# Nyström attention into a squared-ReLU feed-forward: C v on eight tiles, C and A logits on sixteen, C normalised before the product, and a new order

## The chip, the cores and the metric

One core of a Trainium2 chip. The time is device microseconds of one launch; less is better. TensorE is called PE, VectorE DVE, ScalarE ACT, GpSimd POOL and SyncE SP.

## The reference

Eight batches of eight heads, 576 tokens, head width 64. Attention goes through 32 landmarks, the means of 18 tokens each. What it gives is the input of a feed-forward layer (512 to 2048 and back) with a squared ReLU.

```python
q_lm = q.reshape(B, H, 32, 18, D).mean(axis=3)
k_lm = k.reshape(B, H, 32, 18, D).mean(axis=3)
A  = softmax(q    @ k_lm.T / 8)
Bm = softmax(q_lm @ k_lm.T / 8)
C  = softmax(q_lm @ k.T / 8)
Z = Bm.T / (norm_1(Bm) * norm_inf(Bm) + 1e-6)
for _ in range(6):
    Z = 2 * Z - Z @ Bm @ Z
x = A @ Z @ C @ v              # then (4608, 512)
out = square(maximum(x @ w_in, 0)) @ w_out
```

## The kernel before

The whole kernel is a list of operations that a planner in the same file puts in order. Each `op(...)` names the engines that may do it with an estimated duration, what it reads and writes, how many PSUM banks it takes and, for PE, its tile mode. `Plan.schedule` is a list scheduler: it picks on each engine the ready operation with the largest `tail` (the estimated way to the end), with rules for tile modes, PSUM banks (LIMITS) and SP's and POOL's queues. Operations are then issued in the planned order, so every engine runs a fixed queue and waits at its head.

Attention of a batch (`attention(b)`): the landmark sums are matmuls with an identity (L512, mode 64x64), copied from PSUM in two halves (L524) and added (L526); L530 transposes them into LT. L497 transposes K and Q into TT. B (L546, L552 to L585) is softmaxed by small DVE operations. Its column sums, for the norm, are two matmuls with a block pattern (L575) and B B^T is L599 or L603. The six iterations for Z are PE products (L635, L640) and DVE updates (L649), with block diagonals built by POOL or DVE (L589). C's logits are 32 matmuls of 32x32 tiles with 288 columns (L666), its maxima L675, its exponential L681 with the row sums as by-product, its transpose L686. C v is 72 matmuls of 32x64 tiles (L706): four partition groups, each of which uses one of the two column halves. The reciprocals of the row sums (L693, L696) are applied when C v leaves PSUM (L715), which also spreads it block-diagonally. L728 multiplies by Z and L747 by w_in, so that WP = Z C v w_in is copied out by L440 or L444. A's logits (L768), their transposes, softmax (L787 to L804) and the last transpose into AT (L807) complete a batch.

The feed-forward part: `ffn1(b)` multiplies AT by WP in 16 groups of four matmuls with 288 columns (L826), each followed by a ReLU out of PSUM into one of three RS buffers (L839 or L841) and a square into G (L847 or L849). `ffn2` multiplies G by w_out, 16 matmuls of 512 columns for each of 36 tiles of 128 tokens (L861), copies the result into one of three OS buffers and stores it by two DMAs on SP's queue (L876). Until the first L861 matmul, filler matmuls (L952) stand in PE's idle time. Loads are DMAs from POOL's queue (L453, L462, L472, L483) in the order of FIRST_LOADS.

Of the kernel before, what the change touches and what calls it, by code (L numbers as in the profile page):

```python
# [8 lines left out]
P = 128  # L9
# [21 lines left out]


# [5 lines left out]
class Bank:  # L38


    def __init__(self, n, kind):
        self.n, self.kind, self.users, self.at = n, kind, 0, None


class Op:
    __slots__ = ("name", "engs", "emit", "deps", "succ", "tail", "alloc", "uses",
                 "eng", "start", "end", "need", "nbytes", "queue", "seq", "bias", "crit", "unst",
                 "soon", "port", "mode", "ni")


class Plan:
# [5 lines left out]
    BLOCK, FETCH, FETCH_LOADED, PROLOG = 256, 3.8, 6.2, 64  # L57

    SWITCH = 0.092

# [3 lines left out]
    def op(self, name, engs, emit, R=(), W=(), alloc=(), nbytes=0, queue=None, after=(), bias=0.0,  # L64
           crit=False, port=(), mode="full", ni=8):
        o = Op()
        o.crit, o.port, o.mode, o.ni = crit, port, mode, ni
# [57 lines left out]
    def schedule(self, limits):  # L125
# [22 lines left out]

        def banks_for(xs):

            got, taken = [], {}
            for x in xs:
                taken[x.kind] = taken.get(x.kind, held.get(x.kind, 0)) + x.n
# [21 lines left out]
        while done < len(self.ops):  # L175
            moved = True
            while moved:
                moved = False
                for e in ENGINES:
# [3 lines left out]
                    for o in ready[e]:  # L183
                        keep = e == "PE" and o.mode == mode != "full"
# [8 lines left out]
                        if len(o.engs) > 1 and any(  # L193
                                x != e and max(free[x], t) + o.engs[x] + PATIENCE.get(x, 0.0)
                                < t + o.engs[e] + PATIENCE.get(e, 0.0) - 1e-9 for x in o.engs):
                            continue
# [10 lines left out]
                    for x, at in zip(o.alloc, banks_for(o.alloc) if o.alloc else ()):  # L207
                        x.at = at
                        for j in range(x.at, x.at + x.n):
# [16 lines left out]
                    if o.nbytes:  # L226
# [10 lines left out]
                    if o.name[:1] == "O" and e == "PE" and o.name[-1] != "3":  # L237
                        o.end = free[e]
# [59 lines left out]

def v_(n, fast=False):
    return 0.07 + (0.00052 if fast else 0.00104) * n  # L300
# [17 lines left out]
def slot_z(c, r):  # L318
    return pos_c(c, r) % 2

# [17 lines left out]
def kernel(  # L338
# [31 lines left out]
    LS = [mk(f"LS{i}", [P, 256], F32) for i in range(2)]  # L370
    LT = [mk(f"LT{i}", [P, 2, 2, M, 2], BF16) for i in range(2)]
    SAt = [mk(f"SA{u}", [P, 2, 9, M], F32) for u in range(2)]
    Anorm = mk("An", [P, 2, 9, M, 2], BF16)
# [3 lines left out]
    CV = [mk(f"CV{i}", [P, 4, 2, D], BF16) for i in range(2)]  # L377
# [6 lines left out]
    Bb = [mk(f"Bb{i}", [P, 2, M], BF16) for i in range(2)]  # L384
    Blo = [mk(f"Blo{i}", [P, 2, M], BF16) for i in range(2)]
    Bt = [mk(f"Bt{i}", [P, 2, M], BF16) for i in range(2)]
    sm = [mk(f"sm{i}", [P, 18], F32) for i in range(2)]
    smA = [mk(f"smA{u}", [P, 3, 2, 9], F32) for u in range(2)]
# [4 lines left out]
    OS = [mk(f"OS{i}", [P, D_MODEL], F32) for i in range(3)]  # L393
# [3 lines left out]
    ident = mk("ident", [P, P], BF16)  # L397
    msel = mk("msel", [P, 4], F32)
    blk = mk("blk", [P, 4, M], F32)
    blkb = mk("blkb", [P, 4, M], BF16)  # L400
    blk64 = mk("blk64", [P, 4, D], F32)
# [24 lines left out]
    def c_blk(e):  # L426
        nc.vector.tensor_copy(blk[:], msel[:, :].unsqueeze(2).to_broadcast([P, 4, M]))
        nc.vector.tensor_copy(blkb[:], msel[:, :].unsqueeze(2).to_broadcast([P, 4, M]))
        nc.vector.tensor_copy(blk64[:], msel[:, :].unsqueeze(2).to_broadcast([P, 4, D]))
    op("c6", {"DVE": 0.5}, c_blk, R=["msel"], W=["blk", "blkb", "blk64"])  # L430
# [36 lines left out]

    def load_win(z, r, hf):
        c0, c1 = sorted(c for c in range(4) if slot_z(c, r) == z)
# [3 lines left out]
               w_in[64 * z:64 * z + 64, 2 * r:2 * r + 2, 1024 * hf:1024 * hf + 1024],  # L473
               src[:, 4 * r + c0:4 * r + c1 + 1:c1 - c0, :]),
           W=[("win", z, r, hf)], nbytes=524288, queue="sw")

    def at_win(c, r):
        return 2 * r + sorted(x for x in range(4) if slot_z(x, r) == slot_z(c, r)).index(c)
# [8 lines left out]
    def attention(b):  # L487
# [16 lines left out]
        pl_ = Bank(2, "att")  # L504

        def lmx(e, ts):
            o = pair(pl_, 256).rearrange("p j (t r d) -> p j t r d", t=2, r=2)
            for s in range(9):
                for j in range(2):
                    for h in range(2):  # L510
                        i, z = slice(64 * h, 64 * h + 64), 64 * (h ^ j)
                        nc.tensor.matmul(o[z:z + 64, j, ts[0]:ts[-1] + 1],  # L512
                                         lhsT=ident[i, i],
                                         rhs=x[i, ts[0]:ts[-1] + 1, :, 9 * j + s, :],
                                         start=(s == 0), stop=(s == 8))

        for ts in ((1,), (0,)) if b in SPLIT_LM else ((0, 1),):
            op(f"lm{b}.{ts[0]}", {"PE": pe(128 * len(ts), 9) + 0.03}, lambda e, ts=ts: lmx(e, ts),
               R=["ident", *[kx(t, r) for t in ts for r in range(2)]],
               W=[pl_], alloc=[pl_] if ts[-1] == 1 else [], mode="64x64", ni=72)  # L520

        def lmc(e):
            for h in range(2):
                nc.scalar.copy(LS[i2][64 * h:64 * h + 64], bank(pl_, 1)[64 - 64 * h:128 - 64 * h, 0:256])  # L524
        op(f"lmc{b}", {"ACT": 2 * a_(256)}, lmc, R=[pl_], W=[("LS", i2)])
        op(f"lme{b}", {"DVE": v_(256)}, lambda e: nc.vector.tensor_tensor(  # L526
            lm[:].rearrange("p t r d -> p (t r d)"), bank(pl_)[:, 0:256], LS[i2][:], ALU.add),
           R=[pl_, ("LS", i2)], W=[("LM", i2, 0), ("LM", i2, 1)])
        kLT = ("LT", i2)
        op(f"lmt{b}", {"DVE": v_(128)}, lambda e: nc.vector.transpose(  # L530
            lt[:].rearrange("p t r m e -> p (t r m e)").bitcast(U32),
            lm[:].rearrange("p t r d -> p (t r d)").bitcast(U32)),
           R=[("LM", i2, 0), ("LM", i2, 1)], W=[kLT])
# [8 lines left out]
        def sB(e):  # L542
# [6 lines left out]
        op(f"B{b}", {"PE": 0.13}, sB, R=[kLT], W=[pB], alloc=[pB], mode="32x32", ni=32)  # L549
# [14 lines left out]
        op(f"Bmb{b}", {"DVE": 0.14}, lambda e: nc.vector.tensor_tensor(  # L564
            bb[:], bl[:], bc(s_[:, 4:6]), ALU.mult), R=[kb("bl"), kb("brc")], W=[kb("bb")])
        op(f"Btr{b}", {"DVE": 0.09}, lambda e: nc.vector.transpose(
            bt[:].rearrange("p r m -> p (r m)"), bb[:].rearrange("p r m -> p (r m)")),
           R=[kb("bb")], W=[kb("bt")])
        pC = Bank(1, "att")
        op(f"Blo{b}", {"DVE": 0.14}, lambda e: nc.vector.tensor_tensor(  # L570
            blo[:], bf[:], bb[:], ALU.subtract), R=[kb("bf"), kb("bb")], W=[kb("blo")])

        def bcs(e):
            for i, x in enumerate((bb, blo)):
                nc.tensor.matmul(bank(pC)[:, 0:64], lhsT=blkb[:].rearrange("p c m -> p (c m)"),  # L575
                                 rhs=x[:].rearrange("p r m -> p (r m)"),
                                 start=(i == 0), stop=(i == 1))
        op(f"Bcs{b}", {"PE": 0.14}, bcs, R=["blkb", kb("bb"), kb("blo")], W=[pC], alloc=[pC], ni=4)
# [436 lines left out]
```

## Time and profile before

| | |
|---|---|
| median of 3 runs | 273.43 us (272.6 to 273.5) |
| the profiled execution | 272.55 us, its span 270.8 us |
| PE, share of the span | 93% |
| DVE, ACT, POOL | 68%, 76%, 17% |
| granted PE clock | 1.00 throughout |
| first L826 matmul, last L861 matmul | 29.60 us, end at 266.3 us |

The page gives busy time by engine, then the span in 40 slices of 6.8 us in which each digit is a busy share in tenths, and then groups of instructions by line: how many, their busy time, the mean of one, and the idle time of the engine before them. A PE matmul's duration contains the pipeline's latency, so what a group holds of PE is read from the start of one group to the start of the next.

### The profile page before, as it was taken

The numbers are of one execution on the slowest core, as the hardware profiler recorded it, in microseconds if no ns is written. First come the engines' busy times: TensorE is split into PE (matmuls) and PEld (weight loads), VectorE is DVE, ScalarE is ACT, GpSimd is POOL, SyncE is SP. The second block draws the span as 40 slices with busy tenths as digits, with TensorE's granted clock in tenths as the row PEclk, the third lists the DMA queues.
The fourth block names the chain that finished last, engine by engine and source line by source line (L and its number), as shares of the span: only waits on it lengthen the run. The fifth ranks groups of instructions, "written<-read, shape, count | busy, mean of one in ns | idle before, by whom it ended". The sixth has DMA issues, their size and how long they took to land.

```text
span 270.8 us, 7623 instructions
## 1 busy us (share of the span) xinstructions
PE 251.2 (93%) x3132; PEld 139.4 (51%) x3175; DVE 182.8 (68%) x513; ACT 206.3 (76%) x361; POOL 46.7 (17%) x87
## 2 busy tenths in 40 slices
PE   5787789999999999999989999999999999999993
PEld 1434345645664556555745555655645555555441
DVE  2599979999996699669964799358954993000000
ACT  2123895789879799997999989979788999999110
POOL 8445422444070003000300000000000000000000
PEclk9999999999999999999999999999999999999999
DMA  6999999999999815131511111121131111111333
GB/s 110 205 211 209 207 204 213 210 219 249 226 159 203 210 41 92 40 81 39 92 39 41 39 41 41 40 55 36 31 79 40 41 41 40 41 39 41 77 80 77
DMA packets 16100, 28.30 MB, mean 104 GB/s; under 512 B 2240, under 2 KB 4288, under 8 KB 16064
## 3 DMA queue, kind: packets, MB, share of 16 engines
q0 software_dynamic: 10304, 18.35, 37.6%
q1 hardware_dynamic: 5760, 9.44, 14.2%
q8 instruction: 25, 0.41, 0.6%
q14 instruction: 11, 0.09, 0.1%
HBM read 36.70 MB, written 9.44 MB: 170 GB/s over the span
## 4 chain that ended last, share of the span: by engine, by line
PE 63%; ACT 14%; DVE 10%; DMA 6%; issue 4%; POOL 0%; ACTq 0%; DVEq 0%; POOLq 0%
PE ps L861 35%; PE ps L826 18%; DMA X<-in_q_dram 6%; ACT RS L839 5%; ACT G L847 3%; PE ps L747 2%; DVE SA L787 2%; ACT SA L796 2%; PE ps L512 2%; PE ps L666 2%; PE ps L706 1%; DVE SA L794 1%; ACT C L681 1%; PE ps L768 1%; DVE TT L497 1%
## 5 line engine op out<-in xcount | busy, mean ns | idle before, releaser
L861 PE MATMUL ps<-w_out,G 128*128 128x512 bf16 x537 | 136.0, 379 | 3.6 <-issue 1.9
L839 ACT ACTIVATE RS<-ps 128x576 bf16<-128x576 f32 x124 | 77.7, 651 | 14.5 <-PE ps L826 12.6
L826 PE MATMUL ps<-AT,WP 128*128 128x288 bf16 x512 | 79.3, 286 | 2.9 <-ACT RS L839 1.4
L861 PEld LDWEIGHTS <-G 128*128 128x128 bf16 x576 | 52.6, 98 | 49.6 <-issue 4.7
L847 ACT ACTIVATE G<-RS 128x576 bf16<-128x576 bf16 x89 | 60.2, 684 | 1.9
L826 PEld LDWEIGHTS <-WP 128*128 128x128 bf16 x512 | 47.0, 97 | 28.0 <-issue 7.6
L440 ACT COPY OS<-ps 128x512 f32<-128x512 f32 x33 | 19.3, 585 | 15.3 <-PE ps L861 15.1
L849 DVE TENSOR_TENSOR G<-RS 128x576 bf16<-128x576 bf16 x39 | 17.5, 452 | 19.5 <-ACT RS L839 19.3
L497 DVE STREAM_TRANSPOSE TT<-X 128x576 uint32<-128x576 uint32 x32 | 23.8, 756 | 5.3 <-DMA X<-in_k_dram 3.8
L440 ACT CAST WP<-ps 128x1024 bf16<-128x1024 f32 x26 | 25.7, 1011 | 1.6 <-PE ps L747 1.4
L589 POOL TENSOR_TENSOR BD<-ST,blkb 128x256 bf16<-128x256 bf16 x11 | 7.4, 670 | 99.3 <-DVE ST L649 77.3
L462 POOL DMA_DIRECT2D V<-in_v_dram x24 | 12.6, 530 | 45.2 <-PE ps L706 33.6
L681 ACT ACTIVATE C<-ps,sm 128x576 bf16<-128x576 f32 x16 | 14.0, 902 | 5.2 <-DVE sm L678 5.2
L649 DVE SCALAR_TENSOR_TENSOR ST<-ST,ps 128x128 bf16<-128x128 bf16 (+1 forms) x48 | 12.9, 268 | 6.5 <-PE ps L635 6.1
L675 DVE TENSOR_REDUCE sm<-ps 128x1 f32<-128x576 f32 x16 | 11.5, 750 | 6.5 <-PE ps L666 5.9
L524 ACT COPY LS<-ps 64x256 f32<-64x256 f32 x16 | 5.9, 367 | 12.9 <-PE ps L512 11.9
L952 PE MATMUL ps<-onesb 128*128 128x512 bf16 x43 | 12.8, 427 | 1.9 <-DVE onesb L409 1.5
L804 DVE TENSOR_TENSOR An<-SA,smA 128x576 bf16<-128x576 f32 x16 | 12.6, 808 | 0.0
L787 DVE STREAM_TRANSPOSE SA<-ps 128x288 f32<-128x288 f32 x32 | 12.5, 450 | 0.1
L796 ACT ACTIVATE SA<-SA 128x576 f32<-128x576 f32 x16 | 10.5, 679 | 2.2 <-DVE SA L794 2.1
L747 PE MATMUL ps<-w_in,ZC 64*32 64x512 bf16 x256 | 11.7, 383 | 0.3
L798 DVE TENSOR_REDUCE smA<-SA 128x18 f32<-128x576 f32 x16 | 11.7, 747 | 0.0
(78 smaller groups left out, 235.7 us busy)
## 6 DMA issues: line engine op xcount, KB each, us to landing
out_dram<-OS SPq DMA_DIRECT2D x72, 128.0 KB, 2.4
X<-in_k_dram POOLq DMA_DIRECT2D x16, 288.0 KB, 9.7
X<-in_q_dram POOLq DMA_DIRECT2D x16, 288.0 KB, 10.5
V<-in_v_dram POOLq DMA_DIRECT2D x8, 288.0 KB, 8.6
w_in<-in_moe_w_in_dram POOLq DMA_DIRECT2D x8, 256.0 KB, 9.9
w_out<-in_moe_w_out_dram POOLq DMA_DIRECT2D x4, 512.0 KB, 12.3
V<-in_v_dram POOLq DMA_DIRECT2D x8, 216.0 KB, 8.9
V<-in_v_dram POOLq DMA_DIRECT2D x8, 72.0 KB, 8.5
```

Of the source, the lines that this page charges most:

```text
L440: nc.scalar.copy(o, i)
L497: op(f"T{b}.{t}{r}", {"DVE": v_(576)}, lambda e, r=r: nc.vector.transpose(tt[:, t, r].rearrange("p s m e -> p (s m e)").bitcast(U32), x[:, ...
L649: nc.vector.scalar_tensor_tensor(out=o, in0=i0, scalar=2.0, in1=bank(pN)[:, 0:2 * w].rearrange("p (r w) -> p r w", r=2), op0=ALU.mult, op1 ...
L681: op(f"Cex{b}.{r}", {"ACT": a_(576) + 0.27}, lambda e, r=r, pS=pS: nc.scalar.activation(Cs[r][:].rearrange("p x u -> p u x"), pair(pS, HAL ...
L747: nc.tensor.matmul(ps[quad(p), pW.at + z, :], lhsT=ZC[i2][half, p, :], rhs=w_in[half, at_win(c, r), 512 * ch:512 * ch + 512], start=True, ...
L787: nc.vector.transpose(sa[:, r].rearrange("p s m -> p (s m)"), ps[:, pS.at + r, 0:HALF])
L796: op(f"Aex{b}.{u}", {"ACT": a_(576)}, lambda e, sa=sa: nc.scalar.activation(fl(sa), fl(sa), AF.Exp, scale=SCALE / SEG), R=[ksa], W=[ksa])
L826: nc.tensor.matmul(ps[:, ph.at + hf, 0:HALF], lhsT=wp[:, r, 128 * f:128 * f + 128], rhs=at[:, r, HALF * hf:HALF * hf + HALF], start=(r == ...
L839: nc.scalar.activation(o, pair(ph, HALF), AF.Relu)
L847: nc.scalar.activation(G[:, f, base:base + S], RS[i][:], AF.Square)
L849: nc.vector.tensor_tensor(G[:, f, base:base + S], RS[i][:], RS[i][:], ALU.mult)
L861: nc.tensor.matmul(bank(po), lhsT=G[:, f, lo:lo + P], rhs=w_out[:, f, :], start=(f == 0), stop=(f == NF - 1))
```

## The change

- C v runs on both column halves: the first nine positions of each segment on one, the second nine on the other. Both sums are kept, each for its own column half, and added by the next product, whose right-hand side is a masked copy of Z that stands in both halves (ZM, new DVE operations).
- C is divided by its row sums right after the exponential, by ACT or DVE, instead of after C v; the eviction of C v becomes a plain copy by ACT or DVE.
- For batches 2 to 7 (MERGED) C's and A's logits are issued together, two blocks of 32 matmuls, so that all 16 tiles of 32x32 are in use. A's positions are cut into 10 and 8 of a segment's 18 (A_LEN) instead of even and odd ones, and each part has its own AT transpose.
- For batches 2 to 7 (COLS) B's column sums are DVE's: a transpose, a reduction and a transpose back.
- The feed-forward part of batches 0 and 1 (PARTS) is cut at column 320, with 32 groups instead of 16 each; each group takes one PSUM bank. Groups take their banks in the order of the RS buffers (`turn`).
- Landmark sums of batch 0's first half and of batch 1 use the full array (FLAT_LM), 18 matmuls without a second half to add; batch 0's halves are separate, and K and Q are loaded half by half.
- w_in stands in SBUF by head half, the last output tile is cut in two column halves with its final stores on SP's and ACT's queues, and there are five OS buffers.
- The planner has new estimates and rules (`KEEP`, `LANDS`, `turn`, `lean`), and tables that move single operations (URGE, LEAN).

In the order of the new program PE issues in front of its first feed-forward matmul: batch 1's C logits, its column sums and its B B^T as well, and 24 instead of 16 of the w_in products. DVE takes 105 squares (65 of 576 columns, 25 of 320, 15 of 256) instead of 39; ACT takes 55 (31 of 576) instead of 89. PE's fillers are 33 instead of 47.

```diff
+A_LEN = (10, 8)
+N_OS = 5
...
-        def cV(e):
-            for s in range(SEG):
-                for p in range(4):
-                    z = 64 * (p // 2)
-                    nc.tensor.matmul(
-                        bank(pV, p % 2)[z:z + 64, 0:P]
-                        .rearrange("p (r d) -> p r d", r=2),
-                        lhsT=CT[quad(p), s % 9, :, :, s // 9].rearrange("p r m -> p (r m)"), rhs=V[b % 3][quad(p), :, s, :],
-                        start=(s == 0), stop=(s == SEG - 1))
+        def cV(e):
+            for s in range(9):
+                for z in range(2):
+                    for p in range(4):
+                        nc.tensor.matmul(
+                            bank(pVs[p // 2], p % 2)[64 * z:64 * z + 64, 0:P]
+                            .rearrange("p (r d) -> p r d", r=2),
+                            lhsT=CT[quad(p), s, :, :, z].rearrange("p r m -> p (r m)"),
+                            rhs=V[b % 3][quad(p), :, 9 * z + s, :], start=(s == 0), stop=(s == 8))
...
+            op(f"Crc{b}.{r}", {"DVE": 0.16}, lambda e, r=r: nc.vector.reciprocal(
+                s_[:, 14 + r:15 + r], s_[:, 14 + r:15 + r]), R=[kb(f"csm{r}")], W=[kb(f"csm{r}")])
+            op(f"Cnr{b}.{r}", {"DVE": v_(576, True), "ACT": a_(576)}, lambda e, r=r: copy(
+                e, Cs[r][:].rearrange("p x u -> p (x u)"), Cs[r][:].rearrange("p x u -> p (x u)"),
+                scale=s_[:, 14 + r:15 + r]), R=[("C", r), kb(f"csm{r}")], W=[("C", r)], port=("DVE",))
...
+            op(f"Zm{b}.{i}", {"DVE": v_(128, True)}, lambda e, h=h, hs=hs, zs=zs: nc.vector.tensor_tensor(
+                zm[zs, 2 * h:2 * h + 2], zt[hs, :, 1, :].unsqueeze(2).to_broadcast([64, 2, 2, M]),
+                blk2[hs].unsqueeze(1).to_broadcast([64, 2, 2, M]), ALU.mult),
+               R=[kz, "blk2"], W=[(*kzm, i)], port=("DVE",))
...
+        def sCA(e, i):
+            u = i ^ int(pSs[0].at > pSs[1].at)
+            for w in range(2):
+                for r in range(2):
+                    for c in range(4):
+                        mmC(c, r, w, u, pSs[i].at + r)
+                        mmA(c, r, w, i)
...
+        if b in COLS:
+            op(f"Btf{b}", {"DVE": 0.16}, lambda e: nc.vector.transpose(
+                btf[:].rearrange("p r m -> p (r m)"), bf[:].rearrange("p r m -> p (r m)")),
...
+            op(f"Bcs{b}", {"DVE": 0.15}, lambda e: nc.vector.tensor_reduce(
+                s_[:, 16:18], btf[:], axis=AX.X, op=ALU.add), R=[kb("btf")], W=[kb("bcs")])
+            op(f"Bct{b}", {"DVE": 0.16}, lambda e: nc.vector.transpose(
+                bl[:].rearrange("p r m -> p (r m)"), bc(s_[:, 16:18])),
...
-        for f in range(NF):
-            ph = Bank(2, "h")
+        parts = [(0, lens[0]), (lens[0], S)] if b in PARTS else [(0, S)]
+        for u, f in [(u, f) for u in range(len(parts)) for f in range(NF)]:
+            lo, hi = parts[u]
+            nb = 2 if hi - lo == S else 1
+            ph = Bank(nb, "h")
+            ph.turn = rs_n[0]
...
-FIRST_LOADS = [("k", 0), ("q", 0), ("v", 0), ("k", 1), ("q", 1), ("win",), ("v", 1), ("wout",)]
+FIRST_LOADS = [("kq", 0), ("v", 0), ("k", 1), ("q", 1), ("win", 0), ("win", 1), ("v", 1), ("wout",)]
-SPLIT_A = ()
+SPLIT_A = (0,)
+FLAT_LM = ((0, 0), (1, 0))
+MERGED = (2, 3, 4, 5, 6, 7)
+COLS = (2, 3, 4, 5, 6, 7)
+SA_LATE = (0,)
-PATIENCE = {"DVE": 0.4}
+PATIENCE = {"DVE": 0.1}
-URGE = {}
+URGE = {
+    "Ab6": 38.4, "Aex6": -44.7, "Amx0": -90.9, "Amx2": -24.6, "Arc0": -45.9, "Arc1": -36.8,
...
+PARTS = (0, 1)
+KEEP = 1
```

More of the change, by code (lines that the diff above doesn't have):

```diff
@@ L225, in schedule @@
                     o.end = free[e] + self.LAT[e]
-                    if o.nbytes:
+                    if o.queue == "hw":
+                        o.end = free[e] + (self.LANDS_LOADED if queues["sw"] > t else self.LANDS)
+                    elif o.nbytes:
                         q = o.queue
@@ L867, in ffn2 @@
-        i = ti % 3
-        op(f"Oe{ti}", {"ACT": a_(512), "DVE": v_(512) + 0.1},
-           lambda e: copy(e, OS[i][:], bank(po)), R=[po], W=[("OS", i)])
-        def st(e):
-            for j in range(2):
-                b, s = divmod(2 * ti + j, 9)
-                rows = out[b * S:(b + 1) * S, :].rearrange("(m s e) c -> s m e c", s=9, e=2)[s]
-                nc.sync.dma_start(rows, OS[i][64 * j:64 * j + 64, :])
-        op(f"St{ti}", {"SP": 0.7}, st, R=[("OS", i)], W=[], nbytes=262144, queue="hw")
```

461 lines of the change are left out of this document (280 added, 181 removed), and 9 rows, old and new, of the table URGE.

## The prediction

> **What bounds the kernel now.** I read the page first, from the engines' busy time down to the chain that ended last, and then the timeline of the stretches where the change acts.
>
> ```profile
> span 270.8 us, 7623 instructions
> PE 251.2 (93%) x3132; PEld 139.4 (51%) x3175; DVE 182.8 (68%) x513; ACT 206.3 (76%) x361; POOL 46.7 (17%) x87
> PE   5787789999999999999989999999999999999993
> DVE  2599979999996699669964799358954993000000
> ACT  2123895789879799997999989979788999999110
> ...
> PE 63%; ACT 14%; DVE 10%; DMA 6%; issue 4%; POOL 0%; ACTq 0%; DVEq 0%; POOLq 0%
> ...
> L861 PE MATMUL ps<-w_out,G 128*128 128x512 bf16 x537 | 136.0, 379 | 3.6 <-issue 1.9
> L826 PE MATMUL ps<-AT,WP 128*128 128x288 bf16 x512 | 79.3, 286 | 2.9 <-ACT RS L839 1.4
> ```
>
> TensorE (PE) is full from about 30 us to the end, and 63% of the chain that ended last is PE. The two feed-forward products alone need most of it. At the end of the timeline 84 L861 matmuls follow each other in 18.1 us (248.2 to 266.3), 215 ns each; all 576 are 124 us. Eight L826 matmuls hold PE for 0.98 us (126.85 to 127.83), 122 ns each; all 512 are 62.7 us. From the first L826 matmul at 29.60 to the last L861 at 266.3 there are 236.7 us. So 236.7 - 124.1 - 62.7 = 50 us are attention's matmuls, drains and idle time. By the windows PE is busy 211.5 of the 218 us from 30 to 248; 2.0 of the 6.5 idle lie in 30 to 50 us. The change must take its gain from the 50.
>
> ```profile
> 119.40 0.38 PE L861 MATMUL ps<-w_out,G 128*128 128x512 bf16 x1
> 119.71 0.71 PE L666 MATMUL ps<-TT,LT 32*32 32x288 bf16 x32
> 120.35 0.67 PE L826 MATMUL ps<-AT,WP 128*128 128x288 bf16 x4
> ...
> 124.12 0.72 PE L768 MATMUL ps<-TT,LT 32*32 32x288 bf16 x32
> 124.77 0.41 PE L747 MATMUL ps<-w_in,ZC 64*32 64x512 bf16 x8
> ...
> 127.98 1.20 PE L706 MATMUL ps<-V,CT 32*64 32x128 bf16 x72
> 129.11 0.30 PE L826 MATMUL ps<-AT,WP 128*128 128x288 bf16 x1
> ```
>
> These rows of the timeline (start, duration) are batch 4. From one start to the next, C's logits (L666) hold PE for 0.64 us, A's (L768) for 0.65, C v (L706) for 1.13. Streaming explains them: the 32 L666 matmuls go 8 at a time, 4 rounds of 0.122 = 0.49, and 0.15 more; the 72 L706 go 4 at a time, 18 rounds of 0.054 (128 columns at L826's rate) = 0.98, and 0.15 more. So a tiled block costs its rounds plus about 0.15 us.
>
> **The change, part by part.** Savings count on PE after the first feed-forward matmul; before it PE runs fillers.
>
> C v: the same 72 matmuls and loads, now 8 at once in 9 rounds, 0.49 us. Then the loads may pace it: the 16 loads at L546 take 0.14 us (8.75 ns each), 72 would be 0.63; the 72 of L706 take 1.04 us today. With 0.15 for the block that is 0.64 at best, 1.13 at worst. I take 0.75, near the fast loads, because L706's loads today are held back by their matmuls. Gain 0.38 x 7 batches (1 to 7) = 2.7 us, bounds 0 and 3.4 (7 x 0.49).
>
> C and A logits of batches 2 to 7: today 0.64 + 0.65; after, two blocks of 32 with 16 at once. Two rounds of 0.136 (320 columns) or 0.122 are 0.25 to 0.27, 32 loads are 0.28; plus 0.15 each is 0.42, both 0.84. No row shows 16 at once, so the bounds are no gain and that. Gain 0.45 x 6 = 2.7, bounds 0 and 3.6 (without the 0.15 of one block).
>
> B's column sums: two L575 matmuls less in six batches. Their starts lie 0.03 to 0.26 us apart, so 0.1 a batch: 0.6 (0.2 to 1.5). VectorE gets transpose, reduce, transpose for three operations that go; neutral.
>
> Work moved ahead of the first feed-forward matmul: by the order of the new program batch 1's C logits (0.64), its column sums and B B^T (0.25) and one more block of L747's (0.34) now stand among the fillers: 1.2 us. Batch 1's flat landmark sum (18 matmuls of 256 columns, 1.92 us against 1.18) also stands there and costs nothing.
>
> Tile modes: counting runs in the order, PE changes mode 97 times after its first feed-forward matmul today, 86 after. Five of the 11 belong to the moved blocks; six times up to 0.15 is at most 0.9; I take 0.5. Beside that row: the Trainium skill, "TensorEngine Tiling (Array Packing)", Tiling Modes, says that a mode change drains the array. The 0.15 agrees with it; no price of the page is used.
>
> Sum on PE: 2.7 + 2.7 + 0.6 + 1.2 + 0.5 = **7.7 us less**.
>
> Start of the first feed-forward matmul: today 29.60, held by AT (VectorE, 28.80 + 0.75). After, only A's first 320 columns are needed. VectorE is full on the way (9.9 of 10 us between 20 and 30), so I count its queue. Ahead of that transpose it gets batch 1's B softmax (eight operations at 0.13 to 0.2: 1.3), two C maxima of batch 1 (1.42), a transpose of X (0.7), the masked Z (four at about 0.13: 0.5), small ones 0.3; it loses the scaled evictions of C v (0.87), five reciprocals (0.8), a landmark sum (0.3) and half of the AT transpose (0.35). Net 1.9 later. The landmarks come 0.6 earlier: both halves of K and Q land by 10.15 as today, but the copies behind (L524 twice, 0.74 in series) become two of half size side by side. The first weight eviction, which must be there too, ends at 29.15 today and waits for 0.5 of masked Z more. So 30.9: **1.3 us later** (bounds -0.3 and +3).
>
> The first feed-forward batch in two parts: 32 relus instead of 16. From L440 (1024 columns 1011 ns, 512 columns 585) a column costs 0.83 ns, so the relu's 651 ns becomes 0.44 and 0.39: 16 x 0.18 = 2.9 us more on ScalarE, in batches 0 and 1. In batch 0's first part ScalarE needs about 8.7 us (16 relus, a weight eviction, two C v evictions) and PE has some 7; today's loss in 30 to 50 us is 2 us idle. I count no difference (-1 to +3).
>
> Squares: VectorE takes 105 (65 whole) instead of 39, at 452 ns; ScalarE loses 58 whole ones and gets 24 partial at 684 ns for a whole. VectorE rises from 183 to about 202 us, ScalarE falls from 206 to about 188. Both stay under PE, which hides them; VectorE's zeros after 230 us show where the room is.
>
> C normalised early: a reciprocal (0.13) and a scaling (0.45 to 0.68) per half between exponential and transpose, 1.2 us on that path; the scalings after C v go (0.79 and 0.12). Cover: in the timeline C's transpose ends 3.0 to 5.5 us before C v starts in batches 1 to 7 (124.61 to 127.98 in batch 4). If it were gone, PE would wait at the head of its queue, with the feed-forward matmuls behind it.
>
> End: the last copy (0.59) becomes two of 128 columns side by side (L440 ZC, 128 columns, 257 ns), and the last two stores (issued in 1.17 us) go out on two queues: 0.33 + 0.58 at most; I take **0.6 less** (0 to 0.9). The 32 matmuls of 256 columns cost 32 x 0.107 = 3.4, as 16 of 512 do, since a load (98 ns) fits beneath.
>
> Sum: 270.8 - 7.7 + 1.3 - 0.6 = 263.8 us span. The profiled execution took 272.55, 1.75 more than its span, so 265.5. The median of the runs, 273.43, is 0.9 above the profiled one; 0.3% of it, 0.8 us, is about what a measurement of this kernel can tell from no change.
>
> **Rivals.**
>
> Packing gives nothing: 16 tiles share what 8 use today, and the loads pace C v. For it: no row has more than 8 at once, and 72 loads take 1.04 us today. Against it: L666 holds two streams in one row group, and L546's loads show 8.75 ns. Price 5.4 us: 270.9. The Trainium skill, same page, Tile-to-Partition Mapping, says that column tiling turns off fast weight load, which speaks for this rival; the trace has 105 ns for a 32x64 load against 98 for 128x128, so a smaller load is no shorter, but they overlap.
>
> Starved early: between 31 and 60 us VectorE carries attention of batches 1 and 2 plus the squares of the split batch, and the relus wait for free RS buffers (three). For it: VectorE is 9.9 of 10 in 40 to 60 today. Against it: ScalarE gets lighter. Price about 4 us: 269.5.
>
> Slower than before: PE is fed in a fixed order, and C v of a batch stands in it with feed-forward work behind. If C's longer path (Cmx, exponential, reciprocal, scaling, transpose, through a VectorE that now also has the squares) arrives late in every batch, each batch loses the difference. It decides from (7.1 + 0.8) / 7 = 1.1 us a batch beyond the cover, which needs a path 4 to 6 us longer; with 1.5 us a batch, 10.5 us, it is 276. Against it: the cover above.
>
> Less idle: if the rest of PE's 7 us of idle time and the waits at relus shrink by 4, 261.5.
>
> **How the numbers follow.** Forecast 265.5 within about 2.5: 0.56. Packing without gain (one half or both, 268 to 271): 0.12. Starved early (268 to 271): 0.14. Slower mechanism: 0.09. Less idle: 0.09. Bounds at their best (3.4 + 3.6 + 1.5 + 1.2 + 0.9, start -0.3, end 0.9, 3 less idle) give 257.8; the range 259.8 to 271.2 takes in the forecast, most of the faster case, and both rivals on its upper side, and leaves out the slower one. Faster by over 0.3%: 0.88; within: 0.04; slower: 0.08.
>
> **What would show it.** From one start to the next C v at about 0.75 us, the merged logits at about 0.42 each; the first feed-forward matmul near 31 us; PE at 9 in every slice from there to the tail; ACT's busy time near 188, VectorE's near 202; after the last matmul about 3.9 us. It would be wrong if PE's digits fall below 9 in the middle, or if C v's idle time names VectorE.

## The result, and the profile after

The changed kernel takes **268.15 us** (median of 6 runs, 267.66 to 268.86) against 273.25 for the kernel before in runs beside it: ratio 0.9822, 95% interval 0.9801 to 0.9844. It is faster, by 5.1 us where 8 were forecast, and inside the range, though just outside the band of 2.5 us around 265.5. Its profiled execution took 268.4 us, with a span of 266.7. From the page:

```profile
span 266.7 us, 7736 instructions
PE 249.8 (94%) x3129; PEld 138.2 (52%) x3129; DVE 208.2 (78%) x595; ACT 187.2 (70%) x377; POOL 51.3 (19%) x92
PE   5878799999998999998999999999999999999993
DVE  2699999999799769978999789999999965254110
ACT  2054999769876999876698977786675796575430
...
PE 60%; DVE 20%; ACT 8%; issue 5%; DMA 4%; SPq 1%; POOL 1%; DVEq 0%; ACTq 0%; POOLq 0%
...
L928 PE MATMUL ps<-AT,WP 128*128 128x288 bf16 (+2 forms) x512 | 77.1, 286 | 2.1 <-ACT RS L945 1.3
```

In the middle PE's digits fall to 8 in two slices (80 to 87 and 120 to 127 us); the feed-forward matmuls wait for ScalarE's relus as before (2.1 us idle ahead of L928, 2.9 before); ScalarE is lighter (187.2 us, 188 forecast), VectorE heavier (208.2, 202 forecast). L974 is the former L861, L928 the former L826, L798 is C v, L730 and L725 are C's and A's logits. Batch 3's C v and the first merged block of batch 4 in the timeline (start, duration; many single rows of the block are left out):

```profile
110.55 0.83 PE L798 MATMUL ps<-V,CT 32*64 32x128 bf16 x72
111.31 1.04 PE L974 MATMUL ps<-w_out,G 128*128 128x512 bf16 x4
...
128.27 0.30 PE L730 MATMUL ps<-TT,LT 32*32 32x288 bf16 x1
128.28 0.32 PE L725 MATMUL ps<-TT,LT 32*32 32x320 bf16 x1
...
128.42 0.30 PE L730 MATMUL ps<-TT,LT 32*32 32x288 bf16 x3
...
128.71 0.66 PE L928 MATMUL ps<-AT,WP 128*128 128x288 bf16 x4
```

From one start to the next, C v holds PE for 0.76 us (0.75 forecast, 1.13 before), the merged block for 0.44 (0.42 forecast); its matmuls start in two groups, 0.15 us apart. Both sizes came as predicted. But the same timeline has two waits that the old one had not:

```profile
82.67 0.82 PE L798 MATMUL ps<-V,CT 32*64 32x128 bf16 x72 [0.76 <-DVE Bl L593]
...
116.80 3.14 PE L542 MATMUL ps<-X,ident 64*64 64x256 bf16 x107
121.10 0.29 PE L542 MATMUL ps<-X,ident 64*64 64x256 bf16 x1 [1.17 <-issue]
```

C v of batch 2 waits 0.76 us for the PSUM bank that VectorE's L593 frees (C v now needs four banks at once). And the last of 108 landmark matmuls waits 1.17 us for nothing that the profile names. So both signs that the prediction gave for being wrong are there: a digit below 9 in the middle, and a C v whose idle time names VectorE.

### The profile page after: what moved, and what is told of

The parts are those of the page before. It is cut to its first block, busy times and chain, and to the rows that moved or that the text cites. A ratio compares the mean times of both kernels' runs of the same rounds, so it can differ in the third digit from the quotient of the medians.

```text
span 266.7 us, 7736 instructions
## 1 busy us (share of the span) xinstructions
PE 249.8 (94%) x3129; PEld 138.2 (52%) x3129; DVE 208.2 (78%) x595; ACT 187.2 (70%) x377; POOL 51.3 (19%) x92
## 4 chain that ended last, share of the span: by engine, by line
PE 60%; DVE 20%; ACT 8%; issue 5%; DMA 4%; SPq 1%; POOL 1%; DVEq 0%; ACTq 0%; POOLq 0%
PE ps L974 33%; PE ps L928 16%; DVE G L956 4%; PE ps L842 4%; ACT RS L945 3%; DMA X<-in_q_dram 3%; PE ps L542 2%; DVE sm L769 2%; DVE SA L882 2%; ACT C L775 2%; PE ps L798 2%; DVE ST L708 2%; DVE smA L885 2%; DVE smA L893 1%; DVE TT L519 1%
## 5 line engine op out<-in xcount | busy, mean ns | idle before, releaser
L974 PE MATMUL ps<-w_out,G 128*128 128x512 bf16 (+1 forms) x592 | 140.8, 374 | 0.0
L945 ACT ACTIVATE RS<-ps 128x576 bf16<-128x576 f32 (+2 forms) x157 | 79.2, 565 | 21.2 <-PE ps L928 18.8
L974 PEld LDWEIGHTS <-G 128*128 128x128 bf16 x592 | 53.5, 98 | 50.2 <-issue 5.4
L928 PE MATMUL ps<-AT,WP 128*128 128x288 bf16 (+2 forms) x512 | 77.1, 286 | 2.1 <-ACT RS L945 1.3
L928 PEld LDWEIGHTS <-WP 128*128 128x128 bf16 x512 | 48.3, 97 | 29.2 <-issue 6.9
L956 DVE TENSOR_TENSOR G<-RS 128x576 bf16<-128x576 bf16 (+2 forms) x105 | 43.5, 426 | 18.0 <-ACT RS L945 16.7
L954 ACT ACTIVATE G<-RS 128x576 bf16<-128x576 bf16 (+2 forms) x55 | 30.7, 592 | 0.5
L467 ACT CAST WP<-ps 128x1024 bf16<-128x1024 f32 x26 | 25.5, 1018 | 5.5 <-PE ps L842 5.5
L467 ACT COPY OS<-ps 128x512 f32<-128x512 f32 (+2 forms) x32 | 18.1, 571 | 12.6 <-PE ps L974 12.3
L708 DVE SCALAR_TENSOR_TENSOR ST<-ST,ps 128x128 bf16<-128x128 bf16 (+1 forms) x48 | 12.6, 264 | 4.9 <-PE ps L694 4.7
L882 DVE STREAM_TRANSPOSE SA<-ps 128x320 f32<-128x320 f32 (+1 forms) x32 | 13.4, 458 | 1.3 <-PE ps L725 1.3
L899 DVE TENSOR_TENSOR An<-SA,smA 128x640 bf16<-128x640 f32 (+1 forms) x16 | 12.8, 807 | 0.1
L893 DVE TENSOR_REDUCE smA<-SA 128x20 f32<-128x640 f32 (+1 forms) x16 | 11.7, 734 | 0.4 <-ACT SA L891 0.4
L889 DVE TENSOR_TENSOR SA<-SA,smA 128x640 f32<-128x640 f32 (+1 forms) x16 | 11.9, 746 | 0.1
```

The lines of the kernel that those rows point to most:

```text
L467: nc.scalar.copy(o, i)
L708: nc.vector.scalar_tensor_tensor(out=o, in0=i0, scalar=2.0, in1=bank(pN)[:, 0:2 * w].rearrange("p (r w) -> p r w", r=2), op0=ALU.mult, op1 ...
L882: nc.vector.transpose(sa[:, z].rearrange("p s m -> p (s m)"), ps[:, pS.at + z, 0:M * n])
L928: nc.tensor.matmul(ps[:, ph.at + i, 0:w], lhsT=wp[:, r, 128 * f:128 * f + 128], rhs=at[:, r, lo + w * i:lo + w * i + w], start=(r == 0), s ...
L945: nc.scalar.activation(o, x, AF.Relu)
L954: nc.scalar.activation(o, x, AF.Square)
```

## Experiments

All times of this section but the medians and the rows of the timelines are taken **from the first feed-forward matmul on** (30.81 us into the span after, 29.60 before), and each comes from one profiled execution. That start differs by up to 1.5 us between profiled executions of nearly the same beginning, so the medians can't show a step of 0.5 us. Milestones counted from the start repeat within 0.1 us where nothing ahead of them was changed (to F3 84.45 to 84.52 in the changed kernel, e4 and e10). e3 is the exception: with the earliest start it comes to F3 0.26 later, all of it ahead of the first feed-forward matmul of batch 1. F3 and F4 are the first feed-forward matmuls of batches 3 and 4; the stall at the landmarks lies between them, 90 us after the start.

| kernel | to F3 | F3 to F4 | F4 to last matmul | whole | median, us |
|---|---|---|---|---|---|
| changed kernel | 84.52 | 30.79 | 116.30 | 231.61 | 268.15 |
| e1_cv_four | 84.49 | 30.76 | 116.65 | 231.90 | 269.05 |
| e2_ss_eight | 84.44 | 30.01 | 116.54 | 230.99 | 268.09 |
| e3_fill4 | 84.78 | 30.43 | 116.30 | 231.51 | 268.12 (one run) |
| e4_v_late | 84.48 | 29.99 | 116.29 | 230.76 | 268.07 |
| e5_a_same | 85.06 | 30.32 | 117.24 | 232.62 | 269.48 |
| e6_bsb_first | 84.72 | 30.43 | 116.28 | 231.43 | 268.55 (one run) |
| e7_no_scale | 84.18 | 29.49 | 116.37 | 230.04 | 267.50 |
| e8_moves_tail | 84.71 | 30.00 | 116.30 | 231.01 | 267.95 |
| e9_covered | 85.18 | 30.17 | 116.29 | 231.64 | 268.66 |
| e10_cols_two | 84.45 | 29.98 | 116.31 | 230.74 | 268.88 (one run) |
| e11_no_max | 84.50 | 29.61 | 115.57 | 229.68 | 266.26 |
| e12_sq_dve | 84.52 | 29.61 | 115.55 | 229.68 | 266.68 |

The kernel before has 236.71 in all; its order differs too much for the single stretches. My theory at the outset: the savings on PE are real and pay in full, less what new waits take. The rival: the packing gives less than its blocks suggest, since other engines pace the order.

### e1_cv_four: C v's column halves one after the other

```diff
-            for s in range(9):
-                for z in range(2):
+            for z in range(2):
+                for s in range(9):
```

> The changed kernel with the 72 matmuls of C v issued one column half after the other, so that only four tiles of 32x64 work at once, as in the kernel before; the same instructions, the same order, the same PSUM banks. Theory 1 (PE is the bound, a block's time is its rounds): C v holds PE for 1.13 us instead of 0.76 in all eight batches, and the whole time grows by 7 x 0.37 = 2.6 us, to about 270.8. Rival (gains of C v are hidden by other waits): C v grows to 1.13 us but the time by under 1 us.

C v holds PE for 0.97 us instead of 0.76, not the old 1.13 (perhaps the second half starts before the first has drained; no run shows it). So the edit gives back 0.2 us seven times. Up to F3, with three of the seven, nothing of it arrives (84.49 against 84.52); from F4 on, with the last three, 0.35 of 0.6. Ratio to before 0.9834 (0.9816 to 0.9851). A saving on PE is **absorbed in the first 85 us** and arrives, by more than half, behind.

For batch 3 the rows show the place. These are the changed kernel's copy of ZC by ScalarE and the 24 w_in products that read it, then the same two of this run:

```profile
113.31 0.26 ACT L467 CAST ZC<-ps 64x128 bf16<-64x128 f32 x1 [0.34 <-DVE ZC L471]
113.33 1.13 PE L842 MATMUL ps<-w_in,ZC 64*32 64x512 bf16 x24
...
114.36 0.26 ACT L467 CAST ZC<-ps 64x128 bf16<-64x128 f32 x1
114.57 0.95 PE L842 MATMUL ps<-w_in,ZC 64*32 64x512 bf16 x24
```

In both traces the second of the 24 starts 0.05 us after ScalarE's copy has ended, 82.8 us from the first feed-forward matmul. The block holds PE for 1.06 us in the changed kernel, 0.88 here, and 0.77 in batch 4, so PE waits inside it, and with the longer C v it waits less. No idle time of PE is listed there: the second of the 24 starts 0.29 us after the first, whose recorded duration is 0.38. In batch 2 the same block falls from 0.88 to 0.78. For batch 1 no row was found.

### e2_ss_eight: C's 16 matmuls ahead of A's in a merged block

```diff
             for w in range(2):
-                for r in range(2):
-                    for c in range(4):
+                for c in range(4):
+                    for r in range(2):
                         mmC(c, r, w, u, pSs[i].at + r)
+            for w in range(2):
+                for c in range(4):
+                    for r in range(2):
                         mmA(c, r, w, i)
```

> The changed kernel with the merged blocks issued as C's 16 matmuls first and A's 16 after them, so that eight tiles of 32x32 work at once; same instructions, order and banks. Theory 1: each of the 12 blocks holds PE for 0.65 us instead of 0.42, and the time grows by 12 x 0.23 = 2.8 us, to about 271. Rival: it grows by under 1 us, because the logits are waited for elsewhere.

The blocks stay at 0.41 to 0.47 us. The order of issue in a block does not decide how many tiles work at once, so this run does not test the packing. It showed something else: the 1.17 us stall was absent (F3 to F4 30.01), with the landmark matmuls unchanged. So these matmuls do not stall by themselves; why this run had no stall is seen under e4.

### e3_fill4: eight instructions more, early

```diff
+        found[0] = (found[0][0], found[0][1], found[0][2] + 4)
```

> The changed kernel with four more filler matmuls in PE's idle time before 7 us, so that every later PE instruction stands eight places further on. The 1.17 us that PE waits in front of the last of 108 landmark matmuls (121.1 us) is put down to nothing. Theory 2 (PE's instructions come in blocks of 256, and a block came late): the wait stays, about 1.2 us, but four matmuls earlier, in front of the 104th. Rival (it waits for its data or its bank): it stays in front of the 108th. Time as the changed kernel's.

Timeline (its lines lie one lower, L543 is L542):

```profile
116.89 3.03 PE L543 MATMUL ps<-X,ident 64*64 64x256 bf16 x103
120.74 0.40 PE L543 MATMUL ps<-X,ident 64*64 64x256 bf16 x5 [0.82 <-issue]
```

Four fillers with their loads are eight instructions; the wait moves from the 108th to the 104th matmul, four pairs of load and matmul earlier. A wait in batch 1's C logits, shown further down, moves from the 26th to the 22nd. Both stand at a place in the **instruction stream**, not at a datum or a bank.

### e4_v_late: three loads behind the stall

```diff
+        for what, where in [('ldv6.00', 'SS4.0'), ('ldv6.10', 'SS4.0'), ('ldv6.11', 'SS4.0')]:
+            line.remove(at[what])
+            line.insert(line.index(at[where]), at[what])
```

> The changed kernel with the three loads of V for batch 6 issued later on GpSimd's queue, behind its next block diagonal (127.6 us instead of 111.7). In the changed kernel's trace the packet of PE's instructions starts at 118.69 us, when these loads end, though the block before it came at 107.86. Theory 2a (instruction fetch waits behind the load): the fetch comes at about 114 us, the 1.2 us wait in the landmark matmuls goes, and the time falls by about 1.2 us, to 267.0. Rival 2b (PE uses up its instructions faster than they can be fetched, load or not): the wait stays within 0.3 us of 1.2.

```profile
117.76 3.14 PE L542 MATMUL ps<-X,ident 64*64 64x256 bf16 x108
...
122.52 0.65 PE L928 MATMUL ps<-AT,WP 128*128 128x288 bf16 x4 [0.48 <-DVE Bl L593]
```

All 108 follow each other. PE's instruction queue shows why: its packet of 16 KB, which in the changed kernel starts at 118.69 us, behind the three loads issued at 111.71 and among the output's stores, starts at 115.81 here; from the first feed-forward matmul that is 87.9 and 84.0 us. In all seven profiles with the loads in their old place the packet starts within 0.4 us of the end of their last packet, at 86.5 to 88.0; six of them stall, by 0.2 to 1.2 us, and e2, whose loads ended first, does not. In the six with late loads it starts at 84.0 to 84.8, and none stalls. 0.85 us arrive, part of the rest is taken back by the next wait (0.48 for L593). Beside the rows: the Trainium skill, "Runtime: NRT & Kernel Launch", Instruction fetch mechanics, says that the sequencer fetches blocks of 16 KiB, 256 instructions, by its own DMA queue, and that crossing a block is mostly hidden. The size agrees with the packets; here it was not hidden.

### e5_a_same: A's logits on C's eight tiles

```diff
 def pos_a(c, r):
-    return (c + r + 2) % 4
+    return (c + r) % 4
```

> One thing changed: A's logits go to the same eight tiles as C's (tile column c + r instead of c + r + 2), so that a merged block's 32 matmuls find eight tiles and not sixteen; the W product reads its rows from there. Nothing else moves. Theory (packing is what shortens the merged block, and PE's queue passes the saving on): a merged block holds PE for about 0.64 us from one start to the next instead of 0.42, as L666 did before; twelve blocks are 12 x 0.22 = 2.6 us. From the first feed-forward matmul to the last matmul 231.61 becomes 233 to 234.3 (part of it is absorbed up to batch 4, as the four-tile C v showed), the time 269.5 to 270.7. Rival (the merging itself, one block in place of two with two accumulators each, is what saves, and the number of tiles counts for nothing): the blocks stay at 0.41 to 0.46 and the time at 268.1.

The block of above, now:

```profile
128.10 0.34 PE L730 MATMUL ps<-TT,LT 32*32 32x288 bf16 x8
128.24 0.34 PE L725 MATMUL ps<-TT,LT 32*32 32x320 bf16 x8
128.38 0.33 PE L730 MATMUL ps<-TT,LT 32*32 32x288 bf16 x8
128.51 0.34 PE L725 MATMUL ps<-TT,LT 32*32 32x320 bf16 x8
128.78 0.42 PE L928 MATMUL ps<-AT,WP 128*128 128x288 bf16 x2
```

Four rounds of eight, 0.14 us apart, and 0.68 in all: the number of tiles is what saves, so sixteen do work at once in the changed kernel. Of 0.84 us in the four blocks up to F3, 0.54 arrive (up to 0.1 of it may be the early start, 30.70, as in e3); of 1.4 in the six behind F4, 0.94. Ratio to before 0.9868 (0.9849 to 0.9887), 1.3 us slower than the changed kernel.

### e6_bsb_first: the wait at C v of batch 2

```diff
+        for what, where in [('Bsb3', 'Zm2.0')]:
```

> One move on VectorE: batch 3's last eviction of B (L593, which frees the PSUM bank that C v of batch 2 waits for) stands ahead of batch 2's masked-Z operations instead of behind four of them. Theory (C v now takes four banks at once instead of two, and the last of them comes free only when VectorE gets to L593): the 0.76 us that PE waits at C v of batch 2 go, and the milestones behind it come up to 0.8 us earlier; from the first feed-forward matmul to the last 230.9 to 231.2, with part taken back at the waits for masked Z, which now comes about 0.3 us later. Rival (C v waits for its own operands, the transposed C or V): the wait stays at 0.7 or more and names another releaser.

```profile
82.16 0.25 PE L798 MATMUL ps<-V,CT 32*64 32x128 bf16 x3
82.96 0.80 PE L798 MATMUL ps<-V,CT 32*64 32x128 bf16 x69 [0.55 <-ACT OS L467]
...
84.56 0.22 PE L824 MATMUL ps<-ZM,CV 128*128 128x64 bf16 x2
85.04 0.23 PE L824 MATMUL ps<-ZM,CV 128*128 128x64 bf16 x2 [0.25 <-DVE CV L471]
```

L593 holds C v no more, but the next bank does (0.55, ScalarE's copy L467), and 0.25 appear behind. F3 comes 0.2 us **later**. Removing the wait that the profile names brought up the one that ended just before it.

### e7_no_scale: C's scalings left out

```diff
-            op(f"Cnr{b}.{r}", ..., lambda e, r=r: copy(...), ...)
+            op(f"Cnr{b}.{r}", ..., lambda e: None, ...)
```

> C's two scalings by the reciprocal sum ahead of the transpose are left out in every batch (C stays unnormalised, so this kernel leaves out part of the computation). They are 16 operations of 0.45 to 0.68 us on VectorE and ScalarE, about 1.1 us a batch on the way to C v. Theory (the path to C v is covered, so normalising early costs PE nothing): C v holds PE as before, and the time stays within 0.5 us of the changed kernel's 268.15 (267.4 to 268.4), what there is coming from the lighter VectorE. Rival (C's longer path does make PE wait, in the stretch to batch 4 above all, where block savings were seen to be absorbed): from the first feed-forward matmul to the last 231.6 becomes 230 or less, time 266 to 267.

0.34 us less up to F3 and nothing behind F4. Between them 1.30, of which up to 0.98 is the landmark stall (0.19 here): at least 0.3 more. Against e4, which has no stall, the whole is 0.72 less. So the two scalings cost some 0.7 us, and the medians differ by as much (267.50 against 268.15; ratio to before 0.9790, 0.9767 to 0.9814). The time is inside the theory's band, the 230.04 at the rival's edge. The old kernel scaled too, behind C v, so the change itself cost less than that.

### e8_moves_tail: three edits together

The moves of e4 and e6, and the last 256 columns as one copy:

```diff
-            cut = [(c0, c1)] if h == 0 else [(c0, c0 + w // 2), (c0 + w // 2, c1)]
+            cut = [(c0, c1)]
```

> Three edits together, a candidate for a faster kernel: the loads of batch 6's v behind those that follow them on GpSimd (as in the run before, -0.85 us from the first feed-forward matmul to the last), batch 3's eviction of B ahead of the masked Z (-0.4 to -0.8), and the last 256 columns copied by ScalarE in one piece (0.37 us, as the 256 columns just before) instead of 0.27 on ScalarE and 0.29 on VectorE, one after the other and ending 0.58 us after the first began: -0.2 in the tail. Theory (waits of the new order, not the size of the blocks, took the missing 2.6 us): from the first feed-forward matmul to the last 229.8 to 230.4, from the last matmul to the end 4.05, and the time 266.3 to 267.2, ratio to the changed kernel 0.993 to 0.997. Rival (PE is bound by its neighbours there, so a wait removed comes back as the next one): 268.0 within 0.3.

From the last matmul to the end 4.05 us instead of 4.27, as expected of the tail; but 231.01 in place of 229.8 to 230.4, since the move of e6 takes back 0.2. Ratio to before 0.9804 (0.9781 to 0.9828): not to be told from the changed kernel. The rival holds.

### e9_covered: other work ahead of the waits

```diff
+        for what, where in [..., ('O6.1', 'CV2'), ('O6.2', 'ZC2'), ('O6.3', 'W2.0'),
+                            ('O7.0', 'W2.3'), ('O11.3', 'F3.2'), ('O2.2', 'F1.0')]:
```

> The waits are not taken away, the order puts other work in front of them: with the three v loads late and the single last copy as in the run before (and without its move on VectorE), quarters of the second feed-forward product (0.86 us each, their inputs long ready) go ahead of the places where PE was seen to wait: one ahead of C v of batch 2 and one ahead of each of the three steps that follow it, one ahead of the third feed-forward matmul group of batch 3 (waits 0.48 for VectorE L593), one ahead of the first of batch 1 (0.22 for AT). Theory (the missing time is waits that this fixed order brought, each of which can be covered): against the kernel with the late loads alone (230.76) up to 0.76 + 0.48 + 0.22 = 1.46 less from the first feed-forward matmul to the last, 229.3 to 230.1; the milestone at the first feed-forward matmul of batch 3 at 83.5 to 83.9 instead of 84.5; 4.05 behind the last matmul; the time 266.2 to 267.2, ratio to the kernel before 0.974 to 0.978. Rival (ScalarE and VectorE pace this stretch, as the experiment with the move on VectorE suggests: there 0.85 us less at C v of batch 2 came back as new waits before the next milestone): 230.5 to 230.9 and 267.7 to 268.1.

The wait at C v of batch 2 is gone from the timeline, but two of 0.5 and 0.4 stand at batch 1's first feed-forward matmuls, and batch 2's first comes at 57.75 as ever; 1 us behind it PE waits 0.43 for ScalarE's WP (L467), and F3 is 0.7 late. 0.9 us worse than e4. Ratio to before 0.9836 (0.9817 to 0.9856). My theory of single waits fell here.

### e10_cols_two: the price of two small matmuls

```diff
+            if b in COLS:
+                for r in range(2):
+                    nc.tensor.matmul(bank(pY)[:, 0:64], lhsT=BD[1][:, r, :],
+                                     rhs=bt[:].rearrange("p r m -> p (r m)"), start=True, stop=True)
```

> On top of the late v loads, batches 2 to 7 get back what the two column-sum matmuls of B cost PE: two matmuls of 64 columns with 128x128 weights, written to B B^T's bank right ahead of its own, which overwrite them. Twelve matmuls and loads in all, no new wait. Theory (my 0.1 us a batch for them, counted in full): from the first feed-forward matmul to the last 230.76 becomes 231.2 to 231.5. Rival (they slip in beside the neighbours, 64 columns being 0.03 us of streaming each): 230.7 to 230.95. If the instruction block that stalled the landmark matmuls shifts with the two dozen instructions more, a gap at its 108th matmul or a few earlier is to be taken off first.

230.74 against e4's 230.76. The two hold PE for 0.06 us in three of the six batches, and for 0.01 or less in the others. Twelve of them cost nothing that arrives.

### e11_no_max: VectorE 24 us lighter

```diff
-               lambda e, sa=sa, bA=bA: eng(e).tensor_tensor(fl(sa), fl(sa), bA(0), ALU.subtract),
+               lambda e: None,
```

and the same for the maximum (Amx), on top of e4.

> On top of the late v loads, A's softmax is taken without subtracting each row's maximum: the two maxima (0.80 and 0.68 us) and the two subtractions (0.82 and 0.69 us) of every batch go from VectorE, 3.0 us a batch, 24 in all. This leaves out a step of the computation that changes the values only by rounding while the exponentials stay in range (the inputs are small). PE gets the same instructions in the same order. Theory (in the first 110 us VectorE, with ScalarE behind it, paces the fixed order beside PE; that is where the block savings went that did not arrive, and why moving or covering single waits gave nothing): the first feed-forward matmul starts 1 to 2 us earlier, at 28.7 to 30 where the clock is at full speed (then the W evictions on ScalarE hold it), the milestone at the first feed-forward matmul of batch 2, which stood at 57.4 to 58.1 in every run so far, comes at 56 to 57, that of C v of batch 4 at 107 to 108.5 instead of 109.26, from the first feed-forward matmul to the last 228.5 to 230 instead of 230.76; the time 265 to 266.8. Rival (PE itself bounds the stretch and the milestones only look paced): the start alone moves; the milestones behind it stay within 0.2 us of 57.7 and 109.3; the time 266.8 to 267.5.

**266.26 us, ratio to before 0.9744 (0.9715 to 0.9772)**, the fastest of all, at the price named in the expectation. But it is not faster where the theory put it: F3 at 84.50 did not move. All of the 1.08 us against e4 comes behind F3 (0.38 to F4, 0.72 behind). VectorE paces the later stretch in places, and the first not by these operations.

### e12_sq_dve: ScalarE lighter in the first stretch

```diff
+            o.emit("DVE" if o.name in ('Q0.18', ..., 'Q1.29') else o.eng)
```

> On top of the kernel without A's maxima: 14 squares of the split batches (6 of batch 0, 8 of batch 1) go from ScalarE to VectorE, which has had room there since the maxima went. ScalarE loses 14 x 0.36 to 0.46 = 5.7 us, all of it ahead of batch 2's first feed-forward matmul, VectorE gets 14 x 0.27 to 0.32 = 4.1 us. PE's instructions and their order stay. The milestones up to batch 3's first feed-forward matmul (84.50) did not move by 0.03 us when VectorE lost 9 us ahead of them, nor when three C v's ahead of them took 0.2 us more each. Theory (ScalarE paces this stretch: it is busy for 9.5 to 10 of 10 us in 30 to 50, 60 to 70 and 90 to 100): batch 1's first feed-forward matmul at 24.6 or earlier instead of 25.00, batch 2's at 56.5 to 57.3 instead of 57.75, from the first feed-forward matmul to the last 228.9 to 229.4 instead of 229.68, the time 265.5 to 266.0. Rival (neither engine's load, but single hand-overs in the fixed order, PE to VectorE to ScalarE and back, such as the one at C v of batch 2, set the milestones; ScalarE is idle for 4 us in 50 to 60): both milestones within 0.1 us of 25.00 and 57.75, the time 266.0 to 266.5, or more if VectorE, full in 30 to 40, gets late with the squares.

Batch 1's first feed-forward matmul comes at 24.59 instead of 25.00, as the theory has it. But C v of batch 2 is back at 51.90 (51.87), after waits of 0.18 for ScalarE and 0.31 for VectorE's L708. Ratio to before 0.9756 (0.9728 to 0.9784). ScalarE paces the first 25 us. What follows fits the rival, hand-overs between all three engines, but no run separates them.

## Why the prediction was right, and where it was not

**Blocks on PE.** C v 0.75 and logits 0.42 were right in size. For the logits e5 shows the cause, sixteen tiles at once, and for C v e1 shows that the interleaved column halves save. The rival "packing gives nothing" fell. That 0.75 met 0.76 so closely is partly luck: it was a choice between 0.64 and 1.13, and its 8.75 ns a load were read from a row of 16 loads whose 0.14 us contain the last load's own 0.09; they start 3.6 ns apart. In batch 3's C v the last 40 pairs of load and matmul do start 8.3 ns apart; what sets that pace was not tested.

**What failed is the sum's silent step, that the rest of PE's time stays as it is.** 7.7 us less between the first feed-forward matmul and the last were forecast, 5.1 measured. (With the start and the end the sum itself gives 7.0 less; 8 against the median come of starting it at a profiled execution 0.9 below the median.) Where the 2.6 are:
- The landmark stall, 1.17 us; 0.85 arrive when it goes (e4). Shown, with its cause.
- Savings that do not arrive. C v's first three give nothing (e1: PE then waits less for ZC's copies), the last three 0.35 of 0.6; merged blocks two thirds (e5). If what holds for 0.2 us holds for the whole saving, that is 1.1 + 0.4 x 1.5 = 1.7 of C v's 2.6 and 0.9 of the logits' 2.7.
- The column sums: 0.6 forecast, nothing (e10), apart from the waits that stood at the old two.

These come to 0.85 + 1.7 + 0.9 + 0.6 = 4, more than 2.6. So some 1.4 us were gained elsewhere, in waits of the old order or in mode changes, and no run here separates them. The 1.2 us of blocks moved ahead and the 0.5 of mode changes were not tested either. That part stays open.

**The start**: 30.9 forecast, 30.81 measured, with a stall beside the path that I had not foreseen. The chain of events is in these timelines of the changed kernel, PE's and then VectorE's:

```profile
24.52 0.67 PE L730 MATMUL ps<-TT,LT 32*32 32x288 bf16 x25
25.77 0.32 PE L730 MATMUL ps<-TT,LT 32*32 32x288 bf16 x7 [0.58 <-issue]
...
30.47 0.41 PE L842 MATMUL ps<-w_in,ZC 64*32 64x512 bf16 x8 [0.52 <-ACT WP L467]
30.81 0.66 PE L928 MATMUL ps<-AT,WP 128*128 128x320 bf16 x3
...
26.15 0.76 DVE L769 TENSOR_REDUCE sm<-ps 128x1 f32<-128x576 f32 x1
...
30.02 0.51 DVE L902 STREAM_TRANSPOSE AT<-An 128x320 uint32<-128x320 uint32 x1
```

Batch 1's C logits, which the new order put ahead of the first feed-forward matmul, wait in mid-block; the packet of PE's instruction queue starts at 23.46, and they go on 2.3 us later. The landmarks went on 2.4 us after theirs. In this profile the stall holds up nothing: VectorE has no idle time from 19 us to the transpose into AT, and comes to C's first maximum at 26.15, when the logits have just ended (26.09). So its full queue sets the start, as counted, and W's second eviction on ScalarE (1.02 us from 29.39) ends beside the transpose. In eight of the other twelve profiles the stall ends later and VectorE waits for the logits, 0.2 to 0.8 us. e11 is one of them:

```profile
26.82 0.76 DVE L769 TENSOR_REDUCE sm<-ps 128x1 f32<-128x576 f32 x1 [0.28 <-PE ps L730]
```

There 3.0 us of VectorE's work ahead of this had gone, the logits went on at 26.44, and the first feed-forward matmul came at 31.46, the same 5.0 us behind. Queue and stall end nearly together, so lightening the queue alone did not bring the start forward. That the forecast lay within 0.1 us is luck: between the thirteen profiles of the new order the start varies from 30.63 to 32.17.

**C normalised early** was costed at nothing; it is some 0.7 us (e7). **Starved early** was a rival at 14%, by ScalarE's relus or VectorE: as a mechanism it is half right. The changed kernel's waits there are small, but ScalarE paces the first 25 us (e12), and ZC's copies on ScalarE and VectorE take back part of what C v of batches 2 and 3 saves (e1). **Slower** by C's path did not come: C v's one wait names VectorE, but for a bank, not for C's transpose.

**The end**: 0.6 less forecast, 0.27 measured. The two last copies do not lie side by side:

```profile
262.45 0.27 ACT L467 COPY OS<-ps 128x128 f32<-128x128 f32 x1 [1.37 <-PE ps L974]
262.75 0.29 DVE L471 COPY OS<-ps 128x128 f32<-128x128 f32 x1 [8.64 <-DMA out_dram<-OS]
```

VectorE's starts when ScalarE's has ended, so both take 0.59, as the single copy of 512 columns did; one copy of 256 by ScalarE takes 0.37 (e8).

## What to carry to other kernels

Cheaper blocks on the engine that is 93% busy pay in full only where no neighbour paces it: undo a small part of the saving and look at milestones, stretch by stretch, before summing. In a fixed order, the wait that a profile names often hides the next one behind it; moving (e6) or covering (e9) the waits of the first stretch gained nothing, while taking work from VectorE gained 1.1 us in the later ones (e11). A wait that the recorded duration of the matmul before covers is not listed (0.29 us behind a matmul of 0.38, e1): compare how long the same block holds PE in different batches. A dense burst of small matmuls can outrun the fetch of PE's instruction blocks: look for large loads just ahead of it (e4).

## What the runs showed of the hardware

Instruction blocks of 16 KB stalled PE at two places: C's logits of batch 1 in every profile of the changed order (0.2 to 1.4 us), the landmark burst in six (0.2 to 1.2). Matmuls went on 2.2 to 2.4 us after the packet's start. At the landmarks the packet started within 0.4 us of the end of the loads in flight (e4).

In ten of the fourteen profiled executions PE's granted clock fell to half in the first 32 us, where PE runs fillers. Added up from windows of 2 us, it stayed there for 3.4 us in six of them and for 6.8 in four. In e4 (PE busy and its count, PEclk, DMA share, GB/s):

```profile
24.00:26.00 2.00, 0.79 (x42) 1.00 1.13 212
26.00:28.00 2.00, 0.90 (x20) 1.00 1.11 207
28.00:30.00 2.00, 2.00 (x19) 0.50 1.14 216
30.00:32.00 2.00, 1.80 (x29) 0.64 1.13 199
```

PE was busy for less than half of each 2 us before. In the three executions of the changed order without such a stretch the first feed-forward matmul stood at 30.63 to 30.81, in the ten with one at 31.15 to 32.17; whether the one causes the other wasn't tried. The Trainium skill, "TensorE: Matmul & The Clock Gate", Part 1: The HAM clock gate, has the array at half clock after an idle window of about 3.4 us, in windows that run freely, so that the same program meets them differently from run to run. That agrees with the 0.50, with the 3.4 us and twice 3.4, and with its coming and going; but PE was not idle before it here, it was busy for 0.79 and 0.90 of 2 us.
